# Seven block products in place of ten plain sums for two more tile pairs of a dense layer's second projection

## The chip, the cores and the metric

The kernel runs on one core of a Trainium2 chip. Its time is the device time of one execution in microseconds (us); of several runs the median is given. The profile shows one further execution on the same core.

## The reference, cut to what matters

```python
B, S, D, H = 1, 2048, 640, 32          # Dh = 20, F = 1728
g = sigmoid((x * gate_w).sum(-1, keepdims=True))
q, k, v = split(x @ wqkv)
phi = lambda t: concat(softmax(t @ w_phi), softmax(-t @ w_phi))   # per head
a = (phi(q) @ (phi(k).T @ v)) / (phi(q) @ phi(k).sum(0)) @ wo     # per head, then wo
b = silu(x @ w1) @ w2                                             # the dense part
out = g * a + (1 - g) * b
```

Only the dense part b, its gate and its store are touched by the change.

## The kernel before

**Numbers.** Every fp32 operand of a matmul is a pair of fp32r tiles, a high and a low part, and a product is three passes (high by high, high by low, low by high). The high part is a cast on ScalarE, the low part a subtraction on VectorE (DVE) or GpSimd (POOL). One pass over 128 columns of weights and 512 tokens is called a product below; three of them make one block product.

**Tiles and stages.** The 2048 tokens are four blocks of 512 and are worked in two halves, h = 0 and 1, of two blocks (j = 0, 1). The 640 channels are five chunks of 128, the hidden layer is cut into tiles of 128, and two tiles, f and g, are a pair. The stages n = 1 to 10 belong to the dense part: stages 1 to 4 work on the first half, 5 to 9 on the second, stage 10 is the remainder. In stage n TensorE does the first projection of pair n and, between, the second projection of the pair q before it: stage 5 is the one in which the first half's last second projection (q = 4) stands beside the second half's first pair.

**First projection** (`pair_mm`, L1107): the two tiles of a pair by two token blocks are a 2 by 2 block product that is done with seven block products of sums instead of eight. Its steps have the names P1m, P2m, P5m, P4m, P6m, P3m, P7m and Cm with 6, 9, 6, 9, 6, 9, 6 and 3 products, 54 in all; the steps with p (P1p ...) are what the other engines do with the result. PSUM is copied to SBUF (v1, v6 on ScalarE) and combined on DVE (v5, v1, v6, lines L1139, L1140, L1157, L1170, L1171); then `finish` makes silu (ScalarE, L1121), its high part (ScalarE, L1122) and its low part (L1123, DVE or POOL). The results are four u tiles per pair, named u_n_tile_j: u4_9_0 is tile 9, block 0, made in stage 4.

**Second projection** of pair q, in one of two forms. *Ten sums* (`out_items`): for each of two blocks and five output chunks six products into one bank (L1196), 60 in all, and DVE adds the bank to an accumulator in SBUF (L1201). *Sevens* (`sevens`): the two tiles, the two token blocks and the even and odd output chunks 0 to 3 form a 2 by 2 block product that is done with seven block products for each of two pairs of output chunks (a and b): items 1a to 7b, three products each (L1237), and the fifth output chunk plainly, y0 and y1, six products each (L1259); 54 products. It needs sums of the weights (made earlier, kept in HBM, loaded again by `sums_again` as sa tiles of 512 KB), and sums of the silu results, T0 to T3 (`t_sum`, POOL, L1091; high part `t_hi` on ScalarE, L1081; low part `t_lo` on POOL, L1085; the tiles are named ts). A bank is added to more than one accumulator: 16 additions on DVE for one pair (items with an e; L1227, on a first use a copy on ScalarE, L1225). `NSEV` says how many pairs of each half use sevens, (3, 5) before. So stages 1 to 3 and 6 to 10 have them, stages 4 and 5 have ten sums.

**End of the first half.** In stage 5 each finished accumulator is multiplied by its gate on POOL (L1270) and stored (SP, `fb_d`), by `out_store`, after its ten-sum eviction.

**The second half's x.** Its sums of chunks (`x_sum` L1011, `x_part` L1015 and L1016) and its plain chunks (`x_new`: load L733, high part L1530, low part L1531) are made while the first half ends. In the lists, an r is the load of the four raw tiles for the sums, s10 to s41 the sums, p10 to p41 their parts, xl0 to xl4 the loads of plain chunks and xu0 to xu4 their parts. All loads are issued by SP, the sync engine, in order. w0 to w3 (`pair_weights_again`), s0 and s1 (`sums_again`) and c0, c1 (the w2 tiles) are loads that are told to go out after the last x load (`last["x"]`).

**Order.** There is no planner for this part. A list per stage (O1 to O10) names the steps in program order; each step issues its instructions on all engines, and each engine then works in this order and waits by semaphores for data and for tiles that come free.

## Time and profile before

| what | value |
|---|---|
| runs, not profiled | 702.13, 703.97, 705.64 us, median 703.97 |
| profiled execution | 704.52 us, its span 702.6 us |
| granted TensorE clock | 1.00 in the stages below |
| stage 3 (279.10 to 303.60 us of the span) | 24.50 us |
| stage 4 (303.60 to 329.90) | 26.30 us |
| stage 5 (329.90 to 356.20) | 26.30 us |
| stage 6 (356.20 to 380.00) | 23.80 us |

The span runs from the first to the last instruction; times in the trace count from its start. The time of an execution includes about 1.9 us around the span. A row of the profile's groups gives line, engine, operation, output and input tiles, the count, the busy time and mean of one, and the idle time before with what ended it.

### The profile page before, as it was taken

Reading aid. Unit: us, or ns where it says so; the run is one execution under the profiler, and the core shown is the slowest. Engines: PE = TensorE matmul, PEld = TensorE weight load, DVE = VectorE, ACT = ScalarE, POOL = GpSimd, SP = SyncE. Lnnn points to the kernel's source line nnn. Section 1 sums busy time; section 2 is a strip of 40 time slices with the busy share of each in tenths; the row PEclk is TensorE's granted clock in tenths of the full one; section 3 lists DMA queues with packets and bytes.
Section 4 is the critical chain, followed back from the end, with each engine's and each line's share of the span. In section 5 each row is a group of like instructions: output and inputs, shape, how many; then the busy total and the mean of one; then the engine's idle time right before and its main releaser. Section 6 shows DMA issues by size and latency. Waiting matters only on the chain.

```text
span 702.6 us, 11974 instructions
## 1 busy us (share of the span) xinstructions
PE 694.7 (99%) x4536; PEld 589.1 (84%) x4536; DVE 464.4 (66%) x769; ACT 309.4 (44%) x552; POOL 395.5 (56%) x303
## 2 busy tenths in 40 slices
PE   9999999999999999999999999999999989999998
PEld 8888888888888888888888888788988878888878
DVE  4687978887343465677745556567695787888832
ACT  5344555446544433235245233425560754544230
POOL 2376876595662554404695555840499875666332
PEclk9999999999999999999999999999999999999999
DMA  8448888777684577266877444268114366998944
GB/s 307 144 170 293 310 292 298 280 275 237 184 284 146 199 240 231 73 190 240 298 243 245 139 153 126 78 207 261 35 52 140 111 157 202 211 257 209 218 142 132
DMA packets 88631, 140.70 MB, mean 200 GB/s; under 512 B 38466, under 2 KB 52054, under 8 KB 88574
## 3 DMA queue, kind: packets, MB, share of 16 engines
q1 hardware_dynamic: 83134, 132.73, 59.1%
q10 hardware_dynamic: 5440, 7.21, 2.9%
q8 instruction: 36, 0.59, 0.3%
q14 instruction: 21, 0.17, 0.1%
HBM read 87.56 MB, written 45.14 MB: 189 GB/s over the span
## 4 chain that ended last, share of the span: by engine, by line
PE 95%; DMA 2%; DVE 1%; ACT 1%; SPq 0%; issue 0%; DVEq 0%; ACTq 0%
PE kvp L621 18%; PE o L1196 11%; PE o L1237 11%; PE pa L1834 10%; PE a L1107 10%; PE pq L597 9%; PE ph L687 3%; PE b L1107 3%; PE c L1107 3%; PE d L1107 3%; PE o_m L1259 3%; PE pn L1756 2%; PE hp L706 2%; PE kvt L608 2%; DMA oT<-r_d 1%; PE kvp L492 1%
## 5 line engine op out<-in xcount | busy, mean ns | idle before, releaser
L1227 DVE TENSOR_TENSOR acc<-acc,o 128x512 f32<-128x512 f32 x104 | 68.4, 683 | 35.3 <-PE o L1237 35.1
L621 PE MATMUL kvp<-wh,xa 128*128 128x480 f32 (+2 forms) x420 | 90.3, 358 | 0.0
L621 PEld LDWEIGHTS kvp<-wh,xa 128*128 128x128 f32 x420 | 72.8, 188 | 10.0
L1196 PE MATMUL o<-u,w 128*128 128x512 f32 x340 | 80.7, 390 | 0.0
L1834 PE MATMUL pa<-oT,wo 128*128 128x512 f32 (+1 forms) x375 | 73.8, 354 | 2.3 <-DMA oT<-r_d 2.3
L1196 PEld LDWEIGHTS o<-u,w 128*128 128x128 f32 x340 | 63.6, 188 | 13.6 <-DVE acc L1201 0.3
L1834 PEld LDWEIGHTS pa<-oT,wo 128*128 128x128 f32 x375 | 60.5, 191 | 14.0 <-ACT eq L1334 2.3
L1351 POOL TENSOR_TENSOR ez<-eq,zbc 128x1280 f32<-128x1280 f32 x16 | 47.6, 2974 | 22.3 <-ACT eq L1334 17.5
L1123 POOL TENSOR_TENSOR u<-v,u 128x512 fp32r<-128x512 f32 x16 | 20.7, 1296 | 64.0 <-ACT u L1122 64.0
L649 POOL TENSOR_TENSOR ek<-ek,st 128x1280 f32<-128x1280 f32 x16 | 38.3, 2397 | 30.8 <-DVE st L648 18.9
L1121 ACT ACTIVATE v<-v 128x512 f32<-128x512 f32 x33 | 20.9, 632 | 78.2 <-DVE v L1140 36.0
L597 PE MATMUL pq<-wq,xb 128*128 128x320 f32 x360 | 55.1, 310 | 0.0
L597 PEld LDWEIGHTS pq<-wq,xb 128*128 128x128 f32 x360 | 53.3, 188 | 2.0 <-issue 1.5
L1091 POOL TENSOR_TENSOR v<-v,v 128x512 f32<-128x512 f32 x32 | 41.7, 1302 | 13.6 <-DVE u L1123 7.0
L621 PE MATMUL kvp<-wl,xa 128*128 128x480 f32 (+2 forms) x210 | 47.6, 356 | 0.0
L1387 POOL TENSOR_TENSOR eq<-eq,sm 128x1280 f32<-128x1280 f32 x16 | 37.9, 2370 | 15.5 <-DVE sm L1381 15.1
L232 POOL TENSOR_TENSOR xa<-xra,xa 128x512 fp32r<-128x512 f32 (+1 forms) x26 | 28.4, 1114 | 24.1 <-ACT xa L230 17.7
L621 PEld LDWEIGHTS kvp<-wl,xa 128*128 128x128 f32 x210 | 36.6, 188 | 4.8
L1123 DVE TENSOR_TENSOR u<-v,u 128x512 fp32r<-128x512 f32 x25 | 19.9, 798 | 29.6 <-ACT u L1122 28.1
L1107 PE MATMUL a<-xo,wc 128*128 128x512 f32 x132 | 33.5, 389 | 0.0
L1397 ACT COPY ez<-eq 128x2400 uint16<-128x2400 uint16 x10 | 22.0, 2200 | 22.4 <-POOL eq L1387 21.3
L451 ACT COPY v<-kvp 128x340 f32<-128x340 f32 (+1 forms) x30 | 12.4, 423 | 40.8 <-PE kvp L621 22.1
(252 smaller groups left out, 1562.8 us busy)
## 6 DMA issues: line engine op xcount, KB each, us to landing
w<-w_d SPq DMA_DIRECT2D x20, 640.0 KB
w_d<-aw SPq DMA_DIRECT2D x14, 640.0 KB
sa<-s_d SPq DMA_DIRECT2D x16, 512.0 KB
xr<-xT SPq DMA_DIRECT2D x27, 256.0 KB
m_d<-ez ACTq DMA_DIRECT2D x10, 640.0 KB
ra<-w SPq DMA_DIRECT2D x18, 320.0 KB
wb<-w_d SPq DMA_DIRECT2D x9, 640.0 KB
...
```

The source lines that it names most:

```text
L597: nc.tensor.matmul(dst, xt[c][:, hx, :], w[:, c, hw, lo : lo + n], start=first, stop=(hx == 1 and c == NC - 1))
L621: nc.tensor.matmul(kv_cols(t, lo, hi), xt[c][:, hx, :], WKV[hw][:, c, w_cols(lo, hi)], start=(n == 0), stop=(n == 3 * NC - 1), skip_group_ ...
L649: return lambda: nc.gpsimd.tensor_tensor(groups(e), groups(e), spread(st[:, 1, :]), op=ALU.mult)
L1091: nc.gpsimd.tensor_tensor(v[i], v[a], v[b], op=ALU.subtract)
L1107: last["mm"] = nc.tensor.matmul(out, lhs, rhs, start=(first and i == 0), stop=(stop and i == len(todo) - 1), skip_group_check=True)
L1123: eng.tensor_tensor(u[:, 1, :], v, u[:, 0, :].bitcast(F32), op=ALU.subtract)
L1196: nc.tensor.matmul(o, lhs, rhs, start=(n == 0), stop=(n == len(todo) - 1))
L1227: nc.vector.tensor_tensor(acc[j][m], acc[j][m], o, op=ALU.add)
L1237: nc.tensor.matmul(o, ws[hw], x()[hx], start=(first and i == 0), stop=(i == len(PASSES) - 1), skip_group_check=True)
L1351: nc.gpsimd.tensor_tensor(ez, Q[t]["e"], zbc, op=ALU.mult)
L1387: nc.gpsimd.tensor_tensor(groups(q["e"]), groups(q["e"]), spread(q["sm"][:, 2 * H : 4 * H]), op=ALU.mult)
L1834: nc.tensor.matmul(pa[:, a, :], wo_tile[0][:, c, hw, ds], o[:, c, ho, :size], start=(i == 0), stop=(i == len(TERMS) - 1),)
```

## The change

It sets `NSEV` to (5, 5): the second projections of pairs q = 3 and 4 of the first half, in stages 4 and 5, are done by sevens. What follows from it in the code:

- `sevens` gets a flag `end`; a count `left` for each accumulator goes down with each eviction, and in stage 5, where `end` is set, gate and store of an accumulator are issued when its count reaches zero.
- With sevens, the low parts of the first tile's two u tiles are made by POOL and not by DVE, since the call to `finish` chooses the engine by `sev`.
- T tiles: the slots that T0 to T2 had in the first half are also wanted for x chunks 0 to 2 of the second half. Pair 3 keeps them; pair 4 takes new slots (t4_0 and on). The v tiles of stage 3 lie in raw slots.
- All of the second half's plain chunks 0 to 3 are loaded and split in stage 4 (`xl0` to `xl3`, `xu0` to `xu3`), and at other places than before; chunks 0 to 2 were loaded in stage 3 before.
- `last["x"]` is set by loads of the first half's x only, so the loads of w, sa and c no longer stand behind a load of the second half's x.
- Orders O3 to O6 are new.

```diff
-NSEV = (3, 5)
+NSEV = (5, 5)
...
-        last["x"] = nc.sync.dma_start(r, xT[c * P : (c + 1) * P, b * 512 : (b + 1) * 512])
+        i = nc.sync.dma_start(r, xT[c * P : (c + 1) * P, b * 512 : (b + 1) * 512])
+        if b < 2:
+            last["x"] = i
...
-        t = T[q, i] = V[q][4][(i + q) % 2 if i < 2 else i]
+        t = V[q][4][(i + q) % 2 if i < 2 else i]
+        if t is None:
+            t = slot(f"t{q}_{i}")
+            t = [t[:, 0], t[:, 1]]
+        T[q, i] = t
...
-            return raw(f"{name}_{n}")[:, :512] if sev and n in (1, NPAIR, NPAIR + 2) or n == 2 * NPAIR - 2 else v_tile(f"{name}_{n}")
+            return raw(f"{name}_{n}")[:, :512] if sev and n in (1, NPAIR - 3, NPAIR, NPAIR + 2) or n == 2 * NPAIR - 2 else v_tile(f"{name}_{n}")
...
-            V[p] = [v1, None, v6, v5, TS[h]]
+            V[p] = [v1, None, v6, v5, TS[h] if h or p < NPAIR - 2 else [None] * 3 + TS[h][3:]]
...
-    def sevens(q, start):
+    def sevens(q, start, end):
...
+        left = {(j, m): 1 if m == NC - 1 or j and m % 2 == 0 else 2 for j in range(2) for m in range(NC)}
...
             seen.add((j, m))
+            left[j, m] -= 1
+            if end and not left[j, m]:
+                out_store(0, j, m)
...
-            if n != NPAIR - 1 and q < NSEV[n > NPAIR - 1]:
-                sevens(q, n == NPAIR)
+            if q < NSEV[n > NPAIR - 1]:
+                sevens(q, n == NPAIR, n == NPAIR - 1)
...
-                d2 = out_items(int(n > NPAIR - 1), (2 * q, 2 * q + 1), end=n == NPAIR - 1)
+                d2 = out_items(1, (2 * q, 2 * q + 1))
...
-            if n == NPAIR - 3:
-                new_chunks(0, "x", {c: lambda k=k: place(k) for c, k in ((0, 8), (1, 9), (2, 11))})
...
-                new_chunks(0, "x", {4: slot_of(0, 4), 3: lambda: place(10)})
+                new_chunks(0, "x", {c: lambda k=k: place(k) for c, k in ((0, 11), (1, 8), (2, 9), (3, 10))})
+                new_chunks(0, "x", {4: slot_of(0, 4)})
```

The new lists of stage 4, of the start of stage 5 and of the first part of stage 6 (an item with m is its products, with e its evictions):

```
O4 = """
c0 r1 1am t3 t2 P1m t4 h2 P1p l2 P2m P2p h4 w0 l4 c1 r0 xl0 2am 2ae 1ae 2bm 2be 1bm 1be y1m y1e s11
s31 s0 6am 6ae xl1 h3 P5m P5p xl4 l3 P4m s10 5am 6bm y0m s21 6be p10 5bm p11 xl3 w1 y0e P4p 5be 5ae
s30 P6m xl2 s20 xu1 xu0 g w2 w3 xu4 P6p P3m s1 7bm 7am P3p 7ae P7m 4am 7be 4ae 3am s40 P7p s41 4bm
4be 3ae 3bm xu2 xu3 Cm Cp 3be p41 p20 p40 p21
"""
O5 = """
w0 1bm P1m 2am s0 2ae 2bm t3 w1 w2 yl3 P1p s1 2be P2m P2p y1m P5m t2 p31 t4 h3 l3 h2 l2 P5p P4m 1am
...
O6 = """
P1m P1p P2m c0 c1 1bm 1be P2p t3 t2 t4 P5m y1m y1e 2bm w0 y0m y0e h2 l2 P5p P4m P4p 2am 2ae 1am 1ae
h3 s0 l3 h4 P6m P6p 6bm 6am 6ae w1 P3m 6be 5bm 5am 5be s1 7bm 3bm 5ae 7am l4 P3p 3am 2be P7m 3ae 7be
```

**First place: DVE in stage 4**, from the end of P5m on. Before (lines are those of the kernel before):

```order
L1139 TENSOR_TENSOR v5_4_3434<-v1_4_3379,a4_3372 128x512
L1140 TENSOR_TENSOR v1_4_3379<-v1_4_3379,b4_3389 128x512
L1123 TENSOR_TENSOR u4_8_0_3437<-v1_4_3379,u4_8_0_3437 128x512
L1011 TENSOR_TENSOR xr0_0_3383<-xr0_0_3383 128x512
L1201 TENSOR_TENSOR acc0_2_2391<-acc0_2_2391,o0_6_0_2_3443 128x512
L1011 TENSOR_TENSOR xr1_0_3409<-xr1_0_3409 128x512
L1201 TENSOR_TENSOR acc0_3_2392<-acc0_3_2392,o0_6_0_3_3452 128x512
L1201 TENSOR_TENSOR acc0_4_2393<-acc0_4_2393,o0_6_0_4_3481 128x512
L1016 TENSOR_TENSOR xo0_2196<-xr0_0_3383,xo0_2196 128x512
```
After (lines of the new kernel; L1236 is an eviction, L1543 the low part of a plain x chunk, L1020 of a sum of chunks, L1015 the sum):

```order
L1147 TENSOR_TENSOR v5_4_3454<-v1_4_3383,a4_3374 128x512
L1148 TENSOR_TENSOR v1_4_3383<-v1_4_3383,b4_3386 128x512
L1015 TENSOR_TENSOR xr0_0_3405<-xr0_0_3405 128x512
L1236 TENSOR_TENSOR acc0_3_2392<-acc0_3_2392,o3_11_3424 128x512
L1020 TENSOR_TENSOR xo0_2196<-xr0_0_3405,xo0_2196 128x512
L1020 TENSOR_TENSOR xo0_2196<-xr1_0_3362,xo0_2196 128x512
L1236 TENSOR_TENSOR acc0_4_2393<-acc0_4_2393,o3_m0_3481 128x512
L1236 TENSOR_TENSOR acc1_3_2399<-acc1_3_2399,o3_11_3424 128x512
L1236 TENSOR_TENSOR acc1_1_2398<-acc1_1_2398,o3_10_3368 128x512
L1543 TENSOR_TENSOR xo1_2197<-xr2_1_3445,xo1_2197 128x512
L1543 TENSOR_TENSOR xo1_2197<-xr2_0_3411,xo1_2197 128x512
L1543 TENSOR_TENSOR xf_2_4_3523<-xr2_4_3461,xf_2_4_3523 128x512
```
DVE's program has twelve operations between P5m and the v6 add, where there were nine; one low part of u and one sum of chunks have gone; one eviction, one low part of a sum and three low parts of plain chunks have come.

**Second place: DVE at the end of stage 4**, from the v6 add on, the last operations before stage 5's first. Before:

```order
L1157 TENSOR_TENSOR v6_4_3479<-v6_4_3479,c4_3491 128x512
L1123 TENSOR_TENSOR u4_8_1_3512<-v6_4_3479,u4_8_1_3512 128x512
L1201 TENSOR_TENSOR acc1_0_2400<-acc1_0_2400,o0_6_1_0_3503 128x512
L1170 TENSOR_TENSOR v5_4_3434<-v5_4_3434,a4_3372 128x512
L1171 TENSOR_TENSOR v5_4_3434<-v5_4_3434,d4_3459 128x512
L1123 TENSOR_TENSOR u4_9_0_3526<-v5_4_3434,u4_9_0_3526 128x512
L1016 TENSOR_TENSOR xo0_2196<-xr1_0_3409,xo0_2196 128x512
L1016 TENSOR_TENSOR xo1_2197<-xr1_1_3410,xo1_2197 128x512
L1201 TENSOR_TENSOR acc1_1_2398<-acc1_1_2398,o0_6_1_1_3534 128x512
```
After:

```order
L1165 TENSOR_TENSOR v6_4_3526<-v6_4_3526,c4_3528 128x512
L1236 TENSOR_TENSOR acc1_1_2398<-acc1_1_2398,o3_70_3544 128x512
L1236 TENSOR_TENSOR acc1_3_2399<-acc1_3_2399,o3_71_3540 128x512
L1236 TENSOR_TENSOR acc0_1_2390<-acc0_1_2390,o3_70_3544 128x512
L1178 TENSOR_TENSOR v5_4_3454<-v5_4_3454,a4_3374 128x512
L1179 TENSOR_TENSOR v5_4_3454<-v5_4_3454,d4_3464 128x512
L1131 TENSOR_TENSOR u4_9_0_3575<-v5_4_3454,u4_9_0_3575 128x512
L1236 TENSOR_TENSOR acc0_3_2392<-acc0_3_2392,o3_71_3540 128x512
L1236 TENSOR_TENSOR acc1_0_2400<-acc1_0_2400,o3_10_3368 128x512
L1543 TENSOR_TENSOR xo1_2197<-xr2_2_3510,xo1_2197 128x512
L1543 TENSOR_TENSOR xo1_2197<-xr2_3_3497,xo1_2197 128x512
```
The low part of the first tile's second u has gone from here, and the low part of u4_9_0 now has, ahead of it, three evictions and two additions to v5, and behind it two evictions and the low parts of x chunks 2 and 3.

**Third place: POOL at the end of stage 5 and the start of stage 6.** L1270 and L1282 are the gates, L1091 and L1099 the differences, L1085 and L1093 low parts of T tiles. Before:

```order
L1270 TENSOR_TENSOR acc1_1_2398<-acc1_1_2398,G1_1_3370 128x512
L1270 TENSOR_TENSOR acc1_2_2401<-acc1_2_2401,G1_1_3370 128x512
L1270 TENSOR_TENSOR acc1_3_2399<-acc1_3_2399,G1_1_3370 128x512
L1270 TENSOR_TENSOR acc1_4_2397<-acc1_4_2397,G1_1_3370 128x512
L1091 TENSOR_TENSOR v6_5_3724<-v8_5_3806,v6_5_3724 128x512
L1091 TENSOR_TENSOR v8_5_3806<-v8_5_3806,v1_5_3598 128x512
L1091 TENSOR_TENSOR v5_5_3679<-v5_5_3679,v8_5_3806 128x512
L1085 TENSOR_TENSOR ts1_3746<-v8_5_3806,ts1_3746 128x512
L1085 TENSOR_TENSOR ts2_3747<-v6_5_3724,ts2_3747 128x512
L1123 TENSOR_TENSOR u6_2_0_3885<-v1_6_3831,u6_2_0_3885 128x512
```
After:

```order
L1282 TENSOR_TENSOR acc1_3_2399<-acc1_3_2399,G1_1_3519 128x512
L1282 TENSOR_TENSOR acc0_1_2390<-acc0_1_2390,G1_0_3517 128x512
L1282 TENSOR_TENSOR acc0_3_2392<-acc0_3_2392,G1_0_3517 128x512
L1282 TENSOR_TENSOR acc1_2_2401<-acc1_2_2401,G1_1_3519 128x512
L1282 TENSOR_TENSOR acc1_0_2400<-acc1_0_2400,G1_1_3519 128x512
L1099 TENSOR_TENSOR v6_5_3764<-v8_5_3825,v6_5_3764 128x512
L1099 TENSOR_TENSOR v8_5_3825<-v8_5_3825,v1_5_3641 128x512
L1099 TENSOR_TENSOR v5_5_3679<-v5_5_3679,v8_5_3825 128x512
L1093 TENSOR_TENSOR ts1_3793<-v8_5_3825,ts1_3793 128x512
L1131 TENSOR_TENSOR u6_2_0_3911<-v1_6_3851,u6_2_0_3911 128x512
L1093 TENSOR_TENSOR ts2_3794<-v6_5_3764,ts2_3794 128x512
```
One gate more stands ahead of the three differences, and the low part of u6_2_0 now stands between the low parts of ts1 and ts2.

More of the change, by code (lines that the diff above doesn't have):

```diff
@@ L104 @@
 O3 = """
-P1m t3 t2 P1p w0 h2 P2m 2bm c0 s0 h3 2am xl1 xl2 s1 1bm 1am P2p 2ae P5m 1be 1ae 2be y0m P5p c1 w1 xl0
-t4 l2 l3 y0e P4m 6am h4 w2 6bm P4p w3 P6m 6ae l4 6be 5am 5ae y1m y1e 5bm P6p P3m 7am 7bm 5be xu2 3am
-3bm P3p P7m 7ae 4am 7be P7p 4ae 4bm 3be Cm xu1 xu0 3ae Cp 4be
+1bm P1m 1be P1p s0 w0 t3 h3 P2m y1m 2bm 2be t2 h2 l2 1am y1e t4 c0 P2p P5m c1 2am 2ae s1 l3 y0m 1ae
+P5p P4m h4 l4 P4p 6bm 6be 7am P6m P6p 6am y0e w1 6ae P3m P3p 5bm 5be 5am w2 P7m 7bm 5ae 7ae 3am 3bm
+7be 4am 3ae P7p 4bm 4be 3be Cm Cp 4ae w3
 """
 O4 = """
-g P1m P1p c0 r0 P2m o0m o0e c1 r1 P2p o1m w0 o1e P5m P5p w1 s10 o2m o2e s11 o3m P4m P4p s30 o3e s20
-s31 P6m P6p o4m o4e s21 s40 P3m p10 o5m s41 P3p w2 P7m o5e P7p p11 p41 o6m w3 o6e p40 p20 o7m o7e o8m
-xl4 xl3 o8e Cm o9m xu3 Cp p21 xu4 o9e
+c0 r1 1am t3 t2 P1m t4 h2 P1p l2 P2m P2p h4 w0 l4 c1 r0 xl0 2am 2ae 1ae 2bm 2be 1bm 1be y1m y1e s11
+s31 s0 6am 6ae xl1 h3 P5m P5p xl4 l3 P4m s10 5am 6bm y0m s21 6be p10 5bm p11 xl3 w1 y0e P4p 5be 5ae
+s30 P6m xl2 s20 xu1 xu0 g w2 w3 xu4 P6p P3m s1 7bm 7am P3p 7ae P7m 4am 7be 4ae 3am s40 P7p s41 4bm
+4be 3ae 3bm xu2 xu3 Cm Cp 3be p41 p20 p40 p21
 """
 O5 = """
-P1m yl4 P1p p30 p31 o0m o0e yu4 w0 o1m o1e yl2 c0 w1 o2m yu2 o2e P2m o3m P2p P5m yl3 w2 yu3 P5p o3e
-c1 P4m o4m P4p o4e P6m o5m P6p w3 o5e P3m P3p o6m o6e P7m P7p o7m o7e o8m o8e Cm o9m o9e Cp
+w0 1bm P1m 2am s0 2ae 2bm t3 w1 w2 yl3 P1p s1 2be P2m P2p y1m P5m t2 p31 t4 h3 l3 h2 l2 P5p P4m 1am
+y0m y1e 1ae 6am w3 1be c0 yl4 6bm yu3 P4p P6m 6be 5bm yl2 6ae h4 7am l4 y0e yu2 p30 5am yu4 5be P6p
+P3m 5ae 7ae 7bm 3bm P3p P7m 7be P7p 4am 3am Cm 4ae Cp c1 4bm 4be 3be 3ae
 """
 O6 = """
-t3 P1m 2am s0 2ae w0 P1p P2m t2 w1 1bm 1am 1be h2 P2p h3 t4 y0m l2 P5m 2bm s1 1ae c0 2be l3 P5p P4m
-y1m c1 h4 w2 y0e 6am 6bm w3 P4p P6m 6ae l4 6be 5am y1e P6p 5ae P3m 5bm 7am 5be P3p 7ae 7bm 7be P7m
-4am 4ae 4bm 3am 3bm P7p 3ae 3be Cm 4be Cp
+P1m P1p P2m c0 c1 1bm 1be P2p t3 t2 t4 P5m y1m y1e 2bm w0 y0m y0e h2 l2 P5p P4m P4p 2am 2ae 1am 1ae
+h3 s0 l3 h4 P6m P6p 6bm 6am 6ae w1 P3m 6be 5bm 5am 5be s1 7bm 3bm 5ae 7am l4 P3p 3am 2be P7m 3ae 7be
+7ae w2 4bm P7p 4am 4ae 4be 3be Cm Cp w3
 """
```

## The prediction

> **What bounds the kernel now.** I read the profile from the top: the page's busy shares first, then the chain of waits, then the stretches of the four stages that the change rewrites, then single instructions there.
>
> ```profile
> span 702.6 us, 11974 instructions
> PE 694.7 (99%) x4536; PEld 589.1 (84%) x4536; DVE 464.4 (66%) x769; ACT 309.4 (44%) x552; POOL 395.5 (56%) x303
> PEclk9999999999999999999999999999999999999999
> ```
>
> TensorE is busy 694.7 of 702.6 us and its granted clock is full in every slice, so the kernel gets shorter only by fewer or shorter matmuls, or by closing the 7.9 us of gaps. The chain of waits (start, length, what) is TensorE alone around the change:
>
> ```profile
> 318.69 2.04 PE c L1107 x9
> 323.44 4.08 PE o L1196 x18
> 330.93 4.31 PE o L1196 x18
> 355.63 1.36 PE a L1107 x6
> 406.73 2.32 PE o L1237 x9
> 455.88 2.30 PE o L1237 x9
> 476.57 2.36 PE o L1237 x9
> ```
>
> 18 products take 4.08 us when nothing interrupts them: 0.2267 us for one 128x512 product. The same 18 took 4.31 at 330.93, a gap of 0.23 us, the only one in the stages that change. Three later groups of nine took 2.30 to 2.36 instead of 2.04: 0.9 us of gaps there.
>
> Stages 3 to 6 (start:end, length, then busy and count of PE, PEld, DVE, ACT, POOL, clock, DMA share, GB/s):
>
> ```profile
> 279.10:303.60 24.50, 24.50 (x110) 20.30 (x109) 16.39 (x25) 8.18 (x15) 8.52 (x7) 1.00 0.26 88
> 303.60:329.90 26.30, 26.30 (x118) 21.79 (x117) 19.28 (x28) 10.35 (x20) 8.30 (x6) 1.00 0.73 256
> 329.90:356.20 26.30, 26.30 (x117) 21.52 (x116) 19.07 (x30) 11.82 (x22) 15.27 (x11) 1.00 0.79 277
> 356.20:380.00 23.80, 23.80 (x107) 19.71 (x106) 8.91 (x13) 10.60 (x19) 16.89 (x14) 1.00 0.68 227
> sum 100.90, PE 100.90 PEld 83.32 DVE 63.65 ACT 40.95 POOL 48.98; mean PE 25.23 PEld 20.83 DVE 15.91 ACT 10.24 POOL 12.25
> ```
>
> TensorE fills each of them. Stages 4 and 5, which still use ten plain sums, are the long ones; in them DVE works 19 of 26 us and POOL 8 to 15. So there is room beside TensorE now, and the question is whether the change uses it up.
>
> **What the change removes.** A pair's second projection by ten sums is 10 x 6 = 60 products; by seven block products it is 14 x 3 + 2 x 6 = 54. Two pairs: 12 products fewer, all from the engine that bounds. 12 x 0.2267 = **2.72 us**. The gap of 0.23 us belongs to the sums that go: **0.23 us**. Together 2.95 us, and nothing in these four stages can give more, since TensorE has no other gap there.
>
> **What it adds.** For each of the two pairs: six more evictions on DVE (16 for 10); on ACT four casts and on POOL four differences and four low parts, less two low parts that go from DVE to POOL; two loads of 512 KB. Four x chunks move from stages 3 and 4 to stage 4 with all their splitting. DVE in stage 4 goes from 29 operations to 36 (16 evictions for 10, two low parts fewer, three x chunks more), in a stage that shrinks to 108 x 0.2267 = 24.5 us. Unit prices:
>
> ```profile
> L1201 DVE TENSOR_TENSOR acc<-acc,o 128x512 f32<-128x512 f32 x20 | 13.2, 681 | 3.4 <-PE o L1196 3.4
> L1123 DVE TENSOR_TENSOR u<-v,u 128x512 fp32r<-128x512 f32 x12 | 9.9, 826 | 13.4 <-ACT u L1122 12.0 <-POOL xo L1085 1.4
> L1016 DVE TENSOR_TENSOR xo<-xr,xo 128x512 fp32r<-128x512 f32 x8 | 5.5, 724 | 0.0
> L1531 DVE TENSOR_TENSOR xf<-xr,xf 128x512 fp32r<-128x512 f32 x4 | 3.7, 934 | 0.0
> L1011 DVE TENSOR_TENSOR xr<-xr 128x512 f32<-128x512 f32 x2 | 2.1, 1074 | 0.0
> 330.27 1.29 DVE L1016 TENSOR_TENSOR xo<-xr,xo 128x512 fp32r<-128x512 f32 x2
> 322.80 1.73 DVE L1123 TENSOR_TENSOR u<-v,u 128x512 fp32r<-128x512 f32 x1 [1.35 <-ACT u L1122]
> 338.68 1.19 DVE L1531 TENSOR_TENSOR xf<-xr,xf 128x512 fp32r<-128x512 f32 x1
> L1122 ACT CAST u<-v 128x512 fp32r<-128x512 f32 x8 | 5.0, 621 | 0.3
> L1121 ACT ACTIVATE v<-v 128x512 f32<-128x512 f32 x7 | 4.4, 632 | 24.7 <-DVE v L1140 10.9 <-DVE v L1171 7.2 <-DVE v L1157 6.6
> ```
>
> A DVE operation lasts 0.69 us, and two back to back take 1.29, so a full queue moves one per 0.60. Operations that read PSUM always cost that. Those with both inputs in SBUF are sometimes longer: 826, 724, 934 and 1074 ns in the mean, singly 1.19 and 1.73. Over these 26 the excess above 690 is about 0.15 us each while POOL was busy half of the time (48.98 of 100.90). In the new stage 4 POOL has about 16 operations of 1.3 us, 85% of the stage, so I take 0.15 x 0.85 / 0.49 = 0.26 us as an estimate, and 0 and 0.5 (the 1.19 us row) as its ends.
>
> **Price A: DVE between stages 4 and 5.** From the end of P5m to the end of P3m in the new list of stage 4 TensorE has 39 products, 8.84 us. DVE has the twelve operations shown as the first place of the order: 12 x 0.60 = 7.2, 1.64 us to spare; six of them have two SBUF inputs, 6 x 0.26 = 1.6, so it arrives just in time. From P3m's end on, the low part of the third u (u4_9_0) hangs on this path: v6 add 0.69, silu 0.63, cast 0.62, POOL's low part and difference 1.30 each, ScalarE's cast of that difference 0.62, which stands ahead of the next silu, silu 0.63, cast 0.62, low part 0.69: 7.1, with nine hand-overs (v starts 0.03 us after the c group's end: 318.69 + 2.04 = 320.73 against 320.76 in the row below) and the 0.16 by which a product starts before its predecessor ends, 7.5 us. TensorE asks for it after 36 products, 8.16 us: 0.6 us to spare. Then DVE needs 4 x 0.60 = 2.4 us for two evictions and the low parts of two x chunks, which stage 5's P2m asks for nine products (2.04 us) later: 0.3 us left. Three of these operations have two SBUF inputs, 0.8 us: a stall of 0.5. I take **0.6 us**, with the eviction behind them; ends 0 and (10 x 0.5) - 1.64 - 0.3 = 3.1 us.
>
> ```profile
> 320.76 0.69 DVE L1157 TENSOR_TENSOR v<-v,c 128x512 f32<-128x512 f32 x1 [0.43 <-PE c L1107]
> ```
>
> In the old stage DVE waited 0.43 us for c, so this place had no backlog before.
>
> **Price B: POOL at stage 6.** T1 of the next pair (ts) is made on POOL behind the last gates:
>
> ```profile
> 354.86 5.96 POOL L1270 TENSOR_TENSOR acc<-acc,G 128x512 f32<-128x512 f32 x4
> 360.77 4.04 POOL L1091 TENSOR_TENSOR v<-v,v 128x512 f32<-128x512 f32 x3
> 364.77 2.55 POOL L1085 TENSOR_TENSOR ts<-v,ts 128x512 fp32r<-128x512 f32 x2
> L1237 PE MATMUL o<-ts,sa x9: 389/389/389, 367.7 to 370.9; 128*128 128x512 f32 x9
> ```
>
> Before, the first low part ended near 366.1 and TensorE used it at 367.7. Now let R be the start of stage 6. The list of stage 6 puts 60 products ahead of 6bm: 13.6 us, less 0.16. Four gates wait for DVE's last evictions. The first of these stands behind the low part of u5_1_0: P7m ends 12 products (2.7 us) before R, then 0.60 + 0.69 + 0.63 + 0.62 + 0.69 + 0.68 and 0.4 of hand-overs, R + 1.6. ScalarE has a cast ahead of that silu that waits for POOL, by my count of POOL's queue up to 1.4 us more. So R + 1.6 to R + 3.0, and then 5.96 + 4.04 + 1.30: R + 12.9 to R + 14.3 against R + 13.4. I take 0.9 at the late end, 0 at the early one, and with gates at 1.7 instead of 1.49 us each 1.8; value **0.6 us**.
>
> The stores behind the gates cost nothing that I can see: the accumulators they free are overwritten by ScalarE over 2 us later. Queues moved past: in stage 10 the loads of two late x chunks go behind the two sums loads on SP, which had waited for them.
>
> ```profile
> 444.70 10.29 SPq L733 DMA_DIRECT2D xr<-xT  x2
> 455.04 0.90 SPq L1076 DMA_DIRECT2D sa<-s_d  x2
> ```
>
> One of the two x loads held SP 10 us for POOL, and TensorE had no wait for a DMA there, so I cost this at 0; the most it could give is the 0.9 us of later gaps.
>
> **Sum.** -2.72 - 0.23 + 0.6 + 0.6 = -1.75 us. The profiled execution took 704.52 us, 1.9 around its span; the median of the runs shown is 703.97, so 0.55 below it. I apply the sum to the median: **702.2 us** (702.8 for a run like the profiled one).
>
> **Rivals.**
> 1. *The whole gain.* Both places hold, as every such place does in stages 1 to 3 (stage 3 is 24.50 us for 108 products): 703.97 - 2.95 = 701.0. Against it: the margins above are 0.3 us and less.
> 2. *DVE becomes the bound of stage 4.* Every DVE operation with two SBUF inputs takes 1.19 us because POOL is nearly always running: A at 3.1 and B at 1.8, 703.97 - 2.95 + 4.9 = 705.9, slower than before. It decides once DVE loses more than the 1.9 us it has spare over the two stretches, by more than 2.95. For it: the rows of 1.19 and 1.73. Against it: the mean of these rows is far below. [...]
> 3. *The loads come late.* Ahead of the end of P6m ScalarE must cast x chunk 4, in order, and DVE makes its low part ahead of the v6 add. The DMA rows of the stretch from 279 to 330 us, in 40 slices of 1.275 us:
>
> ```profile
> DMA  9951000000003865000008989989999999981000
> GB/s 303 418 215 48 0 0 0 0 0 0 13 0 52 313 163 188 3 0 0 0 0 141 350 287 317 312 217 347 435 420 416 403 400 386 408 343 80 0 0 28
> DMA packets 3054, 8.93 MB, mean 175 GB/s; under 512 B 343, under 2 KB 343, under 8 KB 3050
> ```
>
> By my count of SP's new list 6.5 MB (weights, sums, x chunks 0, 1, 4 and the raw chunks of the gates' half) go out between about 296 and 311 us. At the 0.4 MB/us of the busy slices they are in by 315.5 at the latest; P6m ends 72 products into the stage, 303.6 + 16.3 = 319.9. So 4.4 us are spare, and it decides once the rate stays under 6.5 / (319.9 - 296) = 0.27 MB/us. At 0.2, as in the slices before 312, the last chunk lands 8 us late: 703.97 - 2.95 + 8 = 709.0, slower. Against it: the rate stays above 0.3 as soon as much is queued.
> 4. *More than the whole gain.* The three later gaps, 0.9 us together, close as well because the sums loads no longer stand behind an x load: 703.97 - 2.95 - 0.9 = 700.1. Against it: two of the three stages keep their order, and a gap that DVE or ScalarE makes would stay.
>
> **How the numbers follow.** Chances: the forecast 0.42, rival 1 0.27, rival 2 0.14, rival 3 0.06, rival 4 0.11. What a measurement of this kernel can tell from no change is about 0.5%, 3.5 us (the runs shown go from 702.13 to 705.64). Faster by more, under 700.45: rival 4 and 0.03 of rival 1 for the scatter of the runs, 0.14. Slower by more, over 707.5: rival 3 and 0.03 of rival 2, should stalls of its kind come at more places than two, 0.09. Between, 0.77. The range: below, rival 4 less 0.6 us of scatter (a third of half the spread of 3.5 us), 699.5; above, prices A and B in full, 705.9, and 0.3 of scatter, 706.2. Outside lie rival 3 and a few parts of the others. The forecast's own range is 701.0 to 703.9, between no stall and A alone in full.
>
> **What would show it.** TensorE 12 instructions fewer, stages 4 and 5 at 24.5 us each plus their gaps, and stage 3 as before: the gain. For price A: a gap in stage 5 in front of the product with u4_9_0 or in P2m, with DVE or ScalarE as releaser, and DVE without idle time from the end of stage 4's P5m on. For price B: a gap in front of 6bm in stage 6, released by POOL, and the second low part of ts ending after R + 13.4. Rival 2 would show as means of 1.0 us and more in the groups of DVE with two SBUF inputs; rival 3 as ScalarE or DVE waiting for a DMA of xr in stage 4; rival 4 as nine products in 2.04 us at the three later rows. The prediction is wrong in its reasons if the time comes out near 702 with a stall elsewhere (stage 3's end, where four operations of DVE are ordered anew, or the gates that hold back POOL's low parts in stage 5), and wrong altogether if stages 4 and 5 together last over 52.6 us, their length before.

## The result and the profile after

The changed kernel takes **712.1 us** in the median of four runs (710.48 to 712.72), the kernel before 703.72 on the same occasions: a ratio of 1.0116, 95% interval 1.0098 to 1.0134. It is slower by 8.4 us; the prediction was 702.2, its range ended at 706.2.

The first lines of the profile after:

```profile
span 710.9 us, 12009 instructions
PE 693.5 (98%) x4524; PEld 585.4 (82%) x4524; DVE 477.2 (67%) x777; ACT 314.1 (44%) x560; POOL 423.7 (60%) x323
```

The twelve instructions are gone from TensorE, as the change says. The stretches that answer to stages 4 to 6 (start:end, length, then busy and count of PE, PEld, DVE, ACT, POOL, clock, DMA share, GB/s):

```profile
303.60:329.90 26.30, 24.84 (x110) 20.24 (x109) 21.87 (x30) 10.11 (x18) 17.94 (x14) 1.00 0.89 310
329.90:357.30 27.40, 21.14 (x87) 15.67 (x86) 25.85 (x28) 12.38 (x23) 21.11 (x14) 1.00 0.48 168
357.30:382.00 24.70, 24.17 (x106) 19.29 (x105) 10.71 (x16) 11.95 (x22) 21.15 (x16) 1.00 0.76 233
382.00:387.80 5.80, 5.80 (x27) 4.81 (x26) 2.76 (x4) 3.11 (x6) 3.32 (x3) 1.00 0.82 291
```

Before, the same work and the twelve products filled 76.4 us (303.60 to 380.00), with 0.2 us of gaps. (The counts can't be added up, since a product on a border counts in both rows.) So 7.8 us of the loss lie in these 84.2 us, and TensorE lost 7.8 + 2.72 = 10.5 us to waits. In the second row DVE is busy 25.85 of 27.40 us with two operations fewer than it had in 26.30 us before (30 in 19.07): the operations became longer, not more.

Where TensorE waited (the timeline of its matmuls; in brackets the idle time before a group, and what ended it):

```profile
326.14 0.97 PE L1249 MATMUL o<-xo,w 128*128 128x512 f32 x3 [1.46 <-DVE acc L1236]
332.72 1.61 PE L1249 MATMUL o<-u,w 128*128 128x512 f32 x6 [0.84 <-ACT xo L1542]
336.69 0.96 PE L1115 MATMUL b<-xo,wf 128*128 128x512 f32 x3 [1.18 <-DVE xo L1543]
342.67 1.20 PE L1115 MATMUL d<-xo,wb 128*128 128x512 f32 x4 [1.10 <-DVE xo L1020]
347.81 1.63 PE L1249 MATMUL o<-t,sa 128*128 128x512 f32 x6 [1.22 <-ACT v L1129]
356.14 0.74 PE L1115 MATMUL c<-xf,wf 128*128 128x512 f32 x2 [1.70 <-DVE xf L1543]
377.02 1.43 PE L1249 MATMUL o<-ts,sa 128*128 128x512 f32 x5 [0.52 <-POOL ts L1093]
```

Seven places of half a us and more. The rows name DVE four times, three of these directly with a low part of the second half's x (L1543, L1020). Where they name ScalarE (332.72 and 347.81), its operation had been over for 0.4 and 0.6 us, while an eviction on DVE (L1236) had ended 0.10 us before the product, as the records of the two places show. So DVE ends six of the seven waits. DVE's groups from 303.6 to 359 us (count, busy time, mean in ns):

```profile
L1236 DVE TENSOR_TENSOR acc<-acc,o 128x512 f32<-128x512 f32 x27 | 17.6, 679 | 3.0 <-PE o L1249 2.8
L1020 DVE TENSOR_TENSOR xo<-xr,xo 128x512 fp32r<-128x512 f32 x8 | 10.5, 1356 | 0.0
L1543 DVE TENSOR_TENSOR xo<-xr,xo 128x512 fp32r<-128x512 f32 x4 | 6.4, 1648 | 0.0
L1543 DVE TENSOR_TENSOR xf<-xr,xf 128x512 fp32r<-128x512 f32 x4 | 5.1, 1263 | 0.1
```

The evictions, with one input in PSUM, last 679 ns as before. The sixteen low parts of x, with both inputs in SBUF, take 22.0 us where 16 x 0.69 = 11.0 would do: 11.0 us of excess, beside 10.5 us that TensorE lost. Singly, on DVE and on POOL, from 333 us on:

```profile
333.14 3.50 DVE L1543 TENSOR_TENSOR xo<-xr,xo 128x512 fp32r<-128x512 f32 x2
337.76 5.46 DVE L1020 TENSOR_TENSOR xo<-xr,xo 128x512 fp32r<-128x512 f32 x4
343.14 1.27 DVE L1236 TENSOR_TENSOR acc<-acc,o 128x512 f32<-128x512 f32 x2
```

```profile
331.43 2.98 POOL L1015 TENSOR_TENSOR xr<-xr 128x512 f32<-128x512 f32 x2
334.36 1.72 POOL L1099 TENSOR_TENSOR v<-v,v 128x512 f32<-128x512 f32 x1
337.38 3.00 POOL L1099 TENSOR_TENSOR v<-v,v 128x512 f32<-128x512 f32 x2 [1.30 <-DVE u L1131]
340.41 1.66 POOL L1093 TENSOR_TENSOR t<-v,t 128x512 fp32r<-128x512 f32 x1
```

Two low parts of x in a row take 3.50 us, 1.75 each; POOL's operations beside them 1.7 instead of 1.30. They take turns: a DVE operation that begins while one of POOL's runs ends 0.55 us after that one (0.54 to 0.55 in all nineteen records of this kernel that count as a meeting below), and POOL's next is longer by 0.3 to 0.45 us (1.63 to 1.76 instead of 1.30). Where both queues are full, as in these rows, a pair costs both engines about 1.75 us. Transfers are no part of it; from 338 to 346 us, where the four low parts of the row of 5.46 us ran, the profile has none:

```profile
DMA packets 0, 0.00 MB, mean 0 GB/s; under 512 B 0, under 2 KB 0, under 8 KB 0
```

### The profile page after: what moved, and what is told of

Read it like the earlier page. It is cut to its first block, busy times and chain, and to the rows that moved or that the text cites. A ratio compares the mean times of both kernels' runs of the same rounds, so it can differ in the third digit from the quotient of the medians.

```text
span 710.9 us, 12009 instructions
## 1 busy us (share of the span) xinstructions
PE 693.5 (98%) x4524; PEld 585.4 (82%) x4524; DVE 477.2 (67%) x777; ACT 314.1 (44%) x560; POOL 423.7 (60%) x323
## 4 chain that ended last, share of the span: by engine, by line
PE 87%; DVE 5%; ACT 2%; POOL 2%; DMA 1%; issue 1%; SPq 0%; ACTq 0%; DVEq 0%; POOLq 0%
PE kvp L623 17%; PE o L1249 11%; PE pa L1845 10%; PE pq L599 9%; PE a L1115 8%; PE o L1204 7%; PE ph L689 3%; PE o_m L1271 3%; PE b L1115 3%; PE c L1115 3%; PE d L1115 3%; PE pn L1767 2%; PE hp L708 2%; PE kvt L610 1%; DVE acc L1236 1%
## 5 line engine op out<-in xcount | busy, mean ns | idle before, releaser
L1236 DVE TENSOR_TENSOR acc<-acc,o 128x512 f32<-128x512 f32 x132 | 86.6, 682 | 43.3 <-PE o L1249 36.2
L1131 POOL TENSOR_TENSOR u<-v,u 128x512 fp32r<-128x512 f32 x20 | 26.0, 1299 | 75.5 <-ACT u L1130 75.5
L1099 POOL TENSOR_TENSOR v<-v,v 128x512 f32<-128x512 f32 x40 | 52.8, 1319 | 16.6 <-DVE u L1131 8.4
L1204 PE MATMUL o<-u,w 128*128 128x512 f32 x220 | 51.2, 390 | 0.0
L1204 PEld LDWEIGHTS o<-u,w 128*128 128x128 f32 x220 | 41.2, 188 | 8.6
L1131 DVE TENSOR_TENSOR u<-v,u 128x512 fp32r<-128x512 f32 x23 | 17.3, 754 | 24.8 <-ACT u L1130 23.4
L1249 PE MATMUL o<-u,w 128*128 128x512 f32 x120 | 31.2, 393 | 1.1 <-ACT xo L1542 0.8
```

The source lines that it names most:

```text
L1099: nc.gpsimd.tensor_tensor(v[i], v[a], v[b], op=ALU.subtract)
L1131: eng.tensor_tensor(u[:, 1, :], v, u[:, 0, :].bitcast(F32), op=ALU.subtract)
L1204: nc.tensor.matmul(o, lhs, rhs, start=(n == 0), stop=(n == len(todo) - 1))
L1236: nc.vector.tensor_tensor(acc[j][m], acc[j][m], o, op=ALU.add)
L1249: nc.tensor.matmul(o, ws[hw], x()[hx], start=(first and i == 0), stop=(i == len(PASSES) - 1), skip_group_check=True)
```

## The experiments

The theories, as the expectations name them. *Port theory*: a DVE operation with two SBUF inputs and a POOL operation don't run at the same time; where both queues are full, each pair takes 1.75 us (3.50 us for two at 333.14 above), and DVE is late from there on. It is only a name: the runs show how long operations last beside each other, and no port. *Number theory*: DVE has too many operations, however long each is. *Transfer theory*: the traffic lengthens them. Ratios are to the kernel before, run beside each.

**Idle POOL work in the kernel before.** Nothing of the change; POOL gets twelve operations that nobody reads, where it had been idle from 324 to 337.6 us (T3 stands for two tiles that were not in use then). The idle time stands in brackets in this row of the kernel before:

```profile
337.64 5.09 POOL L1270 TENSOR_TENSOR acc<-acc,G 128x512 f32<-128x512 f32 x3 [13.65 <-DVE acc L1201]
```

```diff
-s31 P6m P6p o4m o4e s21 s40 P3m p10 o5m s41 P3p w2 P7m ...
+s31 P6m P6p o4m o4e s21 s40 P3m p10 o5m s41 P3p z0 z1 ... z11 w2 P7m ...
+ops[f"z{k}"] = lambda: nc.gpsimd.tensor_tensor(T3[0], T3[0], T3[1], op=ALU.subtract)
```

> The kernel before with twelve more POOL subtractions, both inputs and the output in SBUF tiles that nothing uses at that time, in stage 4 behind POOL's last sum of x chunks, where POOL was idle from 324 to 337.6 us. Nothing waits for them except POOL's own queue. Port theory: DVE's operations with two SBUF inputs between 324 and 341 us rise from 0.7 to 0.9 to a mean of 1.4 or more, those with a PSUM input stay at 0.68, the new POOL operations last 1.5 to 1.75 us instead of 1.3, and TensorE gets gaps: 3 to 8 us slower, 707 to 712 us. Number theory and transfer theory: DVE has neither more operations nor more transfers beside it: 0.7 to 0.9 us each, time 703 to 705 us.

Measured: 708.67 us, 1.0099 (1.0074 to 1.0124). From 324 to 348 us:

```profile
L1614 POOL TENSOR_TENSOR xo<-xo,xo 128x512 fp32r<-128x512 f32 x12 | 19.0, 1583 | 0.9
L1016 DVE TENSOR_TENSOR xo<-xr,xo 128x512 fp32r<-128x512 f32 x7 | 10.4, 1515 | 0.0
L1201 DVE TENSOR_TENSOR acc<-acc,o 128x512 f32<-128x512 f32 x8 | 5.3, 674 | 0.0
```

and the same seven and eight operations in the kernel before (324.6 to 342 us):

```profile
L1201 DVE TENSOR_TENSOR acc<-acc,o 128x512 f32<-128x512 f32 x8 | 5.3, 679 | 0.0
L1016 DVE TENSOR_TENSOR xo<-xr,xo 128x512 fp32r<-128x512 f32 x7 | 4.5, 685 | 0.0
```

The low parts go from 685 to 1515 ns, the evictions don't move, the POOL operations last 1583 ns, and TensorE waits 2.09, 1.71 and 1.54 us at three places. DVE had the same operations and the same loads. So POOL's work alone, that nothing waits for, costs 6 to 7 us here. Number and transfer theory fail as an explanation of this.

**Fills in their place.** The same twelve steps write the tile and read nothing.

```diff
-ops[f"z{k}"] = lambda: nc.gpsimd.tensor_tensor(T3[0], T3[0], T3[1], op=ALU.subtract)
+ops[f"z{k}"] = lambda: nc.gpsimd.memset(T3[0], 0.0)
```

> As the run with twelve idle POOL subtractions in the kernel before (1.0% slower), with twelve fills of the same tile in their place: POOL writes SBUF and reads nothing. If DVE is kept out by POOL's reading, DVE's operations with two SBUF inputs stay at 0.7 to 0.95 us and the time at 702 to 704 us; if any POOL operation on SBUF keeps it out for its whole length, they rise as with the subtractions by the length of a fill, and the time by up to 1%.

Measured: 703.25 us, 1.0003 (0.9987 to 1.0019). From 323.3 to 330.4 us, while the fills ran:

```profile
L1614 POOL MEMSET xo<- 128x512 f32 x12 | 6.3, 527 | 0.6
L1016 DVE TENSOR_TENSOR xo<-xr,xo 128x512 fp32r<-128x512 f32 x4 | 2.6, 686 | 0.0
```

The fills, which only write, don't lengthen DVE's operations: four low parts among them at 686 ns, against 1515 among the subtractions, which also read the tile. That the reading makes the difference is my inference, as far as four operations tell.

**The changed kernel without sixteen POOL operations.** This kernel leaves out the six sums of x chunks on POOL and the ten gates.

```diff
 def x_sum(i, r, eng=nc.gpsimd):
+    if eng is nc.gpsimd and r in XR.values():
+        return
...
 def out_store(h, j, m):
-    out_gate(j, m)
+    if h:
+        out_gate(j, m)
```

> The changed kernel without six POOL operations for the sums of x chunks (stage 4) and without the ten gates on POOL (stage 5); the stores stay, DVE does everything that it did. Port theory: the low parts of x on DVE fall from a mean of 1.4 us to below 1.0, the gap near 324 us from 1.6 to below 0.5, all gaps from about 10 us to 3 or less: 702 to 705 us. Number theory and transfer theory: DVE has the same operations and the same loads beside it, so the gaps of stages 4 and 5 stay within a third of what they were: 709 us or more (a gain of at most 2 us from the gates that no longer stand ahead of POOL's low parts in stage 6).

Measured: 705.23 us, 1.0039 (1.0019 to 1.0058), against 1.0116 for the changed kernel. From 303.6 to 378 us:

```profile
L1022 DVE TENSOR_TENSOR xo<-xr,xo 128x512 fp32r<-128x512 f32 x8 | 9.7, 1250 | 0.0
L1546 DVE TENSOR_TENSOR xo<-xr,xo 128x512 fp32r<-128x512 f32 x4 | 3.5, 907 | 0.0
L1546 DVE TENSOR_TENSOR xf<-xr,xf 128x512 fp32r<-128x512 f32 x4 | 3.4, 850 | 0.1
```

DVE does all that it did, and two thirds of the loss are gone. The excess of the sixteen low parts fell from 11.0 to 5.6 us, and TensorE's waits from 10.5 to 4.9. The wait of 1.46 us near 326 and the one at 356 have vanished; so has the one at stage 6, which the gates made. Of those that stay, 1.11 and 1.21 us (339 and 344) stand behind the parts of sums, four of which take 5.45 us here as well, beside POOL's differences for pair 4; the 0.82 us at 330.6 end with the eviction behind the low part of u4_9_0, on the path of price A. The gaps, 4.9 us from start to start of the products, are above the 3 that I expected, since these differences were not left out.

**One SBUF input for DVE.** The low parts of the second half's x become copies of the high parts.

```diff
-nc.vector.tensor_tensor(dst[:, 1, :], r[0], dst[:, 0, :].bitcast(F32), op=ALU.subtract)
+nc.vector.tensor_copy(dst[:, 1, :], dst[:, 0, :])
...
-nc.vector.tensor_tensor(t[:, 1, :], d, t[:, 0, :].bitcast(F32), op=ALU.subtract)
+nc.vector.tensor_copy(t[:, 1, :], t[:, 0, :])    # for the second half
```

> The changed kernel in which the low parts of the second half's x chunks and sums (16 DVE operations with two SBUF inputs in stages 4 and 5, two more later) are plain copies of the high part: same number, same place in the queue, one SBUF input, so the low parts aren't computed. Port theory, if it takes two SBUF inputs: these operations last 0.7 us or less, POOL's operations beside them 1.3 instead of up to 1.75, the gaps of stages 4 and 5 fall from about 10 to below 3 us, 701 to 705 us. If one input on SBUF is enough to meet POOL, they stay at 1.2 us or more and the time at 710 or more. Number theory: the operations are as many, so the gaps stay except for what a shorter copy saves (16 x 0.3 = 5 us at most, if copies take half of the time).

Measured: 706.6 us, 1.0051 (1.0031 to 1.0072). DVE's timeline:

```profile
322.67 0.41 DVE L1546 CAST xf<-xf 128x512 fp32r<-128x512 f32 x1
331.32 2.97 DVE L1546 CAST xo<-xo 128x512 fp32r<-128x512 f32 x2
335.42 4.40 DVE L1021 CAST xo<-xo 128x512 fp32r<-128x512 f32 x4
```

Neither expectation came in whole. A copy alone lasts 0.41 us, and next to POOL's work 0.91 to 1.51 where the timeline shows one singly (347.43 and 348.26): one SBUF input is enough to meet POOL, if it is such a copy. But the copies are 0.28 us shorter (0.41 instead of 0.69), and POOL's operations beside them last 1.46 to 1.50 us instead of 1.63 to 1.76, so the gaps fell to 6.4 us. My "two inputs" was too narrow a description.

**One stage at a time.** Sevens for pair 3 alone, then for pair 4 alone.

```diff
-NSEV = (5, 5)
+NSEV = (4, 5)        # and O5, O6 as before: stage 4 alone
```

```diff
-if q < NSEV[n > NPAIR - 1]:
+if n != NPAIR - 2:   # and O3, O4, x chunks as before: stage 5 alone
```

> Sevens for pair 3 alone (stage 4); stage 5 and 6 have their old lists and ten sums, six products fewer than before (-1.36 us). Port theory (a DVE operation with two SBUF inputs and a POOL operation don't overlap; a pair that meets takes about 1.75 us): the x parts still meet the sums on POOL at the end of stage 4, so the gap near 324 us stays at about 1.6 and the x operations there keep a mean above 1.2; the gaps of stage 5 behind 341 us go, since POOL makes no sums for pair 4. 703.7 - 1.4 + 2 to 4 = 704 to 706.5 us. Number theory (DVE has too many operations, however long each is): stage 4 keeps its 36 and loses about as much as in the changed kernel up to 341 us, 5.8 us: 708 us. Transfer theory (the DMA traffic at the end of stage 4 lengthens DVE's operations): the loads there are the same, 708 us.

> Sevens for pair 4 alone (stage 5), stages 3 and 4 with their old lists, old places of the x chunks and ten sums in stage 4 (-1.36 us). Port theory: the x parts that DVE makes between 324 and 341 us, where POOL had nothing to do before, now meet POOL's differences and low parts for pair 4: mean of these DVE operations 1.2 or more, gaps in stage 5 of 3 to 5 us, 705 to 708 us. Number theory: DVE has stage 4 as before, so no stall ahead of stage 5, and half of stage 5's: about 704 to 705 us. Transfer theory: the transfers of stage 4 are those of before, DVE operations at 0.7 to 0.9 us, 703 us.

Measured: stage 4 alone 708.86 us, 1.0089 (1.0067 to 1.0111); stage 5 alone 705.32, 1.0050 (1.0031 to 1.0069). The second is where port theory had it, but only 0.3 us above number theory's end, which four runs don't tell apart; its waits are 1.32, 1.16 and 0.53 us, but its low parts of x, 0.86 and 1.14 us in the mean, met POOL less than I expected. The first is not; it is near number theory's 708, but for another reason: TensorE waited 3.3 us at 325 (busy for 0.38 of 3.70) and then ran at a granted clock of 0.55 (columns as above):

```profile
325.00:328.70 3.70, 0.38 (x2) 0.00 (x0) 2.36 (x5) 1.25 (x2) 0.00 (x0) 1.00 0.85 226
328.70:332.50 3.80, 3.77 (x10) 2.98 (x11) 2.55 (x4) 0.23 (x1) 0.00 (x0) 0.55 0.68 265
```

My edit had caused that itself: without sevens for pair 4, the low parts of its u tiles go to DVE, in a list that was made for POOL; DVE then waits for a cast, with the evictions behind. With these low parts on POOL:

```diff
-finish((f, 0), v1, eng=nc.gpsimd if sev else nc.vector)
+finish((f, 0), v1, eng=nc.gpsimd if sev or n == NPAIR - 2 else nc.vector)   # also for (f, 1)
```

> Sevens for pair 3 alone, as in the first run, but with the low parts of the first tile's two u tiles of stage 4 on POOL, as the new list of stage 4 expects it: in the first run they stood on DVE and the product after P7m's start waited 3.5 us for the evictions behind them. Port theory: the gap near 325 us falls from 3.5 us to about 1.6, as in the changed kernel, the slow products behind it go, stage 5 has small gaps only: 704 to 707 us. Number theory: DVE has two operations fewer, 1.2 us: 706 to 708 us.

Measured: 704.86 us, 1.0014 (0.9999 to 1.0029), as port theory had it. One wait of 1.64 us is left at 326, and 0.24 at 343. From 330.6 to 339 us POOL has nothing to do, and DVE does six parts of sums in 3.69 us:

```profile
321.28 2.96 DVE L1542 TENSOR_TENSOR xo<-xr,xo 128x512 fp32r<-128x512 f32 x2
334.70 3.69 DVE L1019 TENSOR_TENSOR xo<-xr,xo 128x512 fp32r<-128x512 f32 x6
```

Two operations beside POOL's sums take 2.96 us, six without POOL 3.69. Both rows are of this one kernel.

**Moving POOL's work to DVE.** The six sums of x chunks, then the ten gates too, in the changed kernel:

```diff
-eng = nc.vector if i == 1 else nc.gpsimd
+eng = nc.vector
```

```diff
-out_gate(j, m)
+out_gate(j, m, nc.gpsimd if h else nc.vector)
```

> The changed kernel with the six sums of x chunks of the second half that POOL makes in stage 4 on DVE, at the same places of the lists. Port theory: DVE gets six operations more (3.6 us) but no longer meets those six (up to 6 x 1.06 us), the low parts near 321 to 335 us last 0.7 to 1.0 us: a little faster than the changed kernel, 708 to 711 us. Number theory: DVE was the bound by its count, six more cost up to 3.6 us: 713 to 716 us.

> As the run before, and the ten gates of the first half on DVE too, each right behind the accumulator's last eviction. Port theory: sixteen POOL operations (24 us of POOL) become sixteen of DVE at 0.6 us (10 us); DVE meets POOL only for differences and low parts of u and T; 704 to 709 us, faster than the changed kernel. Number theory: DVE has sixteen operations more, 715 us or more.

Measured: 712.59 us, 1.0145 (1.0118 to 1.0172), and 712.25, 1.0134 (1.0112 to 1.0155): no better than the changed kernel. Port theory had 708 to 711 and 704 to 709, number theory 713 to 716 and 715 or more; neither came in, though the first time is only 0.4 us under number theory's. Some operations did get shorter (the low parts of chunks 0 to 3 from 1648 to 761 ns in the first, 760 in the second), others didn't (the parts of sums, 1435 and 1297 after 1356), since POOL's differences still ran beside them. And DVE has the operations that it takes over to do (686 and 760 ns for a sum, 926 for a gate in the mean of the second run), and it is full. A part of both times is a slower clock, told at the end: 1.6 us in the first and, as an estimate from the row there (5.88 us of products at half speed), some 2.5 in the second. Without it TensorE's waits are 9.5 and about 10 us, against 10.5. So the number of DVE's operations does matter, once the line has no idle time: neither theory holds alone.

The same in the kernel with sevens in stage 5 alone, where DVE has idle time: the sums, both, the gates.

> Sevens for pair 4 alone, and the six sums of x chunks that POOL makes in stage 4 on DVE, which has 29 operations there and idle time. The low part of u4_8_1 and the first difference for pair 4 wait for these six on POOL now (its queue was full from 314 to 324 us). Port theory: the low parts of x chunks at 328 us meet POOL less, the gap of 1.5 us there closes or halves: 703.5 to 705 us (705.3 without the edit). Number theory: six DVE operations more in stage 4, same or slower, 705 to 708 us.

> As the run before, and the ten gates on DVE too, behind the last evictions. Port theory: the low parts of x near 345 to 350 us no longer meet gates and POOL's differences for stage 6 no longer stand behind gates: the gaps at 348 (1.3 us) and 370 (0.7 us) close, at ten DVE operations of 0.6 us more in a stage with DVE 3/4 busy: 701 to 704 us, faster than both stage 5 variants, and at best 1.4 us under the kernel before. Number theory: sixteen DVE operations more, 706 us or more.

> Sevens for pair 4 alone and the ten gates on DVE, the sums on POOL as they were. Both theories as for the two runs before, one edit at a time: port theory 703 to 705 us (the gap at 328 stays, those at 348 and 370 close), number theory 706 us or more.

Measured: 705.39 us, 1.0036 (1.0019 to 1.0053); 706.48, 1.0045 (1.0028 to 1.0062); 706.91, 1.0049 (1.0035 to 1.0062), beside 1.0050 without. The gain that I forecast didn't come; the three times lie in number theory's ranges, and the intervals don't tell them from the run without these edits. With both edits the eight parts of sums last 690 ns each and the wait at 370 is gone, but others take their place:

```profile
330.53 0.96 PE L1248 MATMUL o<-u,w 128*128 128x512 f32 x3 [1.23 <-DVE acc L1208]
344.85 0.96 PE L1248 MATMUL o<-t,sa 128*128 128x512 f32 x3 [0.93 <-DVE acc L1235]
```

The second follows gates that stand between evictions on DVE. The first is the path of price A: on the chain of waits POOL's difference (L1098, to 326.1) releases ScalarE's cast, behind which stand silu and cast for the third u, then DVE's low part at 328.0. It doesn't depend on the sums.

**Moving two splits behind the v6 addition**, in the kernel with sevens in stage 4 alone and in the changed kernel.

```diff
-... s20 xu1 xu0 g w2 w3 xu4 P6p P3m s1 7bm 7am P3p 7ae P7m 4am 7be 4ae 3am ...
+... s20 xu1 g w2 w3 P6p P3m s1 7bm 7am P3p 7ae P7m 4am 7be xu0 4ae xu4 3am ...
```

> Sevens for pair 3 alone with the low parts of u on POOL (0.14% above the kernel before, one gap of 1.8 us at 324 us), and in stage 4's list the splits of x chunks 0 and 4 behind the v6 addition and its first evictions instead of ahead of them; chunk 1 stays ahead. Port theory: the two low parts that met sums on POOL no longer stand ahead of the v6 addition, the gap at 324 us closes to 0.3 us or less, and behind it DVE has idle time from 326 to 331: time 1.4 to 1.8 us lower than without the move, level with the kernel before or up to 0.2% under it (702 to 703.5 on a before of 703.4). Number theory: DVE has as many operations, the gap moves to the start of stage 5: no change, 704.5 to 705.5.

> The same move in the changed kernel, with sevens in both stages. If DVE and POOL together are full from 317 to 359 us there (the excess of the operations that meet, 12 us), the gap at 324 us closes but those from 331 to 354 grow by as much: 711 to 712.5 us. If the order ahead of the v6 addition alone were at fault, 710 us or less.

Measured: 704.58 us, 1.0015 (0.9999 to 1.0032), and 713.72, 1.0149 (1.0118 to 1.0179). In the first the wait at 326 is gone and one of nearly the same length stands a little later, since the v5 additions, which free a bank for TensorE, are now behind the two splits:

```profile
327.78 0.96 PE L1114 MATMUL a<-xf,wb 128*128 128x512 f32 x3 [1.38 <-DVE v L1177]
342.95 1.65 PE L1114 MATMUL a<-xo,wc 128*128 128x512 f32 x6 [0.56 <-DVE v L1146]
```

My expectation of a gain failed, and the one that number theory gave (no change, 704.5 to 705.5) came in. DVE has no room at this place, and the excess is only handed on. In the second kernel the move made a wait of its own, 4.59 us: ScalarE's cast for x chunk 0 came to stand behind a cast that waits for POOL's difference. It says nothing on the question.

## Why the prediction was wrong

**What held.** The twelve products went and are worth what was said: 4536 to 4524 instructions, 2.72 us. Price B, POOL at stage 6: the wait in front of the first product with ts is there, released by POOL, 0.52 us on the timeline, 0.68 from start to start, against 0.6; without the gates it is not there. Some of that closeness is luck, since five gates of 7.22 us in all stood there and not the four of 5.96. The place of price A was right too: TensorE waits at u4_9_0's product and in P2m of stage 5 (rows of 332.72 and 336.69), and from the v6 addition the low part of u4_9_0 took 7.2 us (324.81 to 332.02) against 7.5. Rival 3 (loads) played no part.

**What failed is the unit price of price A**, in the step that took 0.26 us as the excess of a DVE operation with two SBUF inputs, with 0.5 us as its upper end. It measured 0.69 us in the mean of the sixteen low parts (1.37 instead of 0.69) and up to 1.1 singly. The step averaged the excess over 26 operations and scaled it with POOL's share of the time. But the excess isn't spread evenly. In the records of both kernels (low parts and x sums on DVE, 250 to 490 us), an operation that begins while a POOL subtraction, multiplication or addition has more than 0.15 us to run ends 0.55 us after it; all others last 0.68 to 0.70 us. So the excess is anything from nothing to 1.1 us (the longest low part, L1543, lasted 1.81), by how much of POOL's operation is left. The kernel before has 37 operations without such a meeting and nine with one, 1.16 us in the mean, 1.73 at most. After, it is 21 and 19, and the nineteen have 1.35. In the kernel before POOL was idle from 324 to 337.6 us, just where DVE split most of the x chunks; that was no accident of the mean, but what made the old stages fit. The change put POOL's differences for pair 4 into that time, and three more splits ahead of it.

The row that should have set the upper end was quoted: 1.73 us for the low part at 322.80. It was passed over for the 1.19 row. With (1.73 - 0.69) for ten operations, price A's upper end would have been 10 x 1.04 - 1.64 - 0.3 = 8.5 us, and the range's 701.0 + 8.5 + 1.8 + 0.3 = 711.6, close below the 712.1 that came. That would have been near by luck, since the stretches of price A lost less than that and others lost the rest.

**A second failure: DVE's time to spare.** The sum gave DVE 1.64 us to spare from P5m's end to P3m's end, as if its queue never waited. DVE's timeline there:

```profile
316.57 0.69 DVE L1236 TENSOR_TENSOR acc<-acc,o 128x512 f32<-128x512 f32 x1 [1.29 <-PE o L1249]
317.17 2.46 DVE L1020 TENSOR_TENSOR xo<-xr,xo 128x512 fp32r<-128x512 f32 x2
321.35 2.94 DVE L1543 TENSOR_TENSOR xo<-xr,xo 128x512 fp32r<-128x512 f32 x2
324.81 0.68 DVE L1165 TENSOR_TENSOR v<-v,c 128x512 f32<-128x512 f32 x1
```

It stood idle for 1.29 us, for a product (6bm), and that used up most of the 1.64. The two pairs of low parts had 2.8 us of excess, where the sum had 1.6 and as its upper end 3.0. The v6 addition, which was to come just in time at P3m's end (321.97), began 2.8 us after it. The first and in this stretch only wait of TensorE, at 326.14, is this delay.

**A third failure: two places.** The sum charged the stall once and let DVE catch up. DVE had 1.9 us to spare over two stretches; once it was behind, the same excess came again in stage 5 (the sums' parts at 342, chunks at 356), in stretches that I had not costed. From start to start of the products, TensorE lost 4.7 us in the stretches of price A (the sum had 0.6), 5.0 in stretches without a price, and 0.8 at price B.

**The rivals.** Rival 2 (DVE becomes the bound) was the mechanism, and got 0.14 and a price of 4.9 us; the loss was 10.5. What it had against it, that the mean of the rows is far below 1.19 us, was the wrong measure: the operations that met POOL at all had 0.47 us over in the mean before (1.16 - 0.69) and 0.66 after (1.35 - 0.69). Rival 4 is refuted, since the three later waits stayed as they were (chain of waits, after):

```profile
414.53 2.32 PE o L1249 x9
463.66 2.31 PE o L1249 x9
484.35 2.34 PE o L1249 x9
```

**How the 10.5 us divide** is settled only in part. Without sixteen of POOL's operations about two thirds of the loss go, with shorter DVE operations somewhat more than half; taking over POOL's operations takes at most 1 us off the waits and nothing off the time. The loss comes from both together: DVE has little idle time in these stages, and the meetings use up 11 us. How much of it the six more evictions per pair would cost with POOL quiet was not measured. No version here is faster than the kernel before; with sevens in stage 4 alone it is level within the interval.

## What to carry to other kernels

Where VectorE and GpSimd both work on SBUF, sort the operations of one by whether the other was running when they began, before taking a mean: here the price ran from nothing to 1.1 us beside a GpSimd operation of 1.3 us, by where in it they began, and a mean scaled by a share of busy time missed it. Idle time of GpSimd next to VectorE's operations with two SBUF inputs was cover in use here (13.65 us in the kernel before, and 6 to 7 us lost with subtractions in it); before filling such time, charge what a pair took here, 1.75 us with tiles of 128x512, for each pair that will meet, and carry the lateness through all later stretches until an engine shows idle time. The upper end of a price must be the worst single row, not the second worst. And time to spare that is worked out from a queue's operations holds only where the queue doesn't wait.
